# Attention units that own a pair of PSUM banks, batch 0 put into the mixing's tiles, and a priority for every group of operations

## The chip, the cores and the metric

The kernel runs on one core of one Trainium2 chip. The metric is the device time of one execution in microseconds. Three runs of the kernel before took 1059.05, 1060.00 and 1061.12 us, a median of 1060.0 us. The profiled execution took 1059.67 us and its trace spans 1057.9 us; times inside the trace count from the start of that span.

## What is computed

The reference does attention with two kinds of masks, and then a layer that mixes along the sequence and the channels and ends in a feed-forward part. Cut to what matters:

```python
batch, n_heads, seq, head_dim = (8, 8, 576, 64)
# heads 0-3: the last 32 rows; heads 4-7 ("dilated"): every 4th of the last 128 rows
mask_plain = (rel >= 0) & (rel < 32)
mask_dil   = (rel >= 0) & (rel < 128) & (rel % 4 == 0)
x = softmax(where(mask, q @ k.T / 8, -1e9)) @ v          # -> [8, 576, 512]

mixed = real(fft(fft(x, axis=1), axis=2))                # sequence, then channels
u  = x + mixed
un = (u - mean(u)) / sqrt(var(u) + 1e-6)
out = u + maximum(un @ w_ch1, 0) @ w_ch2                 # 512 -> 2048 -> 512
```

## The kernel before

The program is one stream of small operations for TensorE (PE), VectorE (DVE), ScalarE (ACT), GpSimd (POOL) and the DMA queue that SyncE (SP) issues. It has two halves. In the first, about 594 us long, attention, mixing and the feed-forward part of the first six of sixteen blocks of 128 hidden columns run mixed together. In the second, the other ten blocks are done for all tokens by a scheme with seven products in place of eight (`product`, `down7`).

**Attention.** `attention` takes a batch, and in it first the plain heads and then the dilated heads. For each, `loads` brings the keys (`kb`) and the queries (`tq`), and `attend` works through five units `u`: four whole ones of two pairs of heads by four groups of 32 rows, and one half as large. A unit is a chain: scores on PE (L668), masking with the row's extreme on DVE (L677), exponentials on ACT (L683), transposes on PE (L688), a copy to SBUF on ACT (L693), the values on PE (L699), then sum, reciprocal and scaling on DVE (L711, L713, L715) into a tile `xt`, which `store` sends to two DRAM tensors, `xsp` and `xsm` (forward rows and rows counted from the end). All units share the same two banks, held in `split`: the scores of successive units take turns in columns 0 to 127 and 128 to 255, and every unit's values go to columns 256 and up. The transposes take turns in two more banks, `pt` and `av`. In numbers of whole units, a batch has nine and the program 72.

**Mixing.** `mix` does one batch. Its `fold` loads the batch's rows from `xsp` and `xsm` into tiles `x` and `xt` (L802, L811), adds and subtracts them (POOL L814 and L816, DVE L828 and L830, ACT L832 and L833, POOL L836 and L838). Then follow products along the sequence (L865, L887) and along the channels (L911, L917), sums and differences on DVE (L925, L927), the addition of `x` on POOL (`add_u`, L779 and L781), `normalise` (DVE L744 to L756 with a power on POOL L750), and for batch 0 transposes on PE (L764). The result is a tile `ut` of 256 tokens.

**Feed-forward part of the first half.** `fill` takes such a tile through six hidden blocks: `up` (PE L1089, then ACT L1095 and DVE L1097 make `h`), and `down` (PE L1105). There are 18 such tiles, so 108 hidden tiles `h`, each of 12 products up and 6 products down. Their weights arrive as 64-bit floats and are taken apart by `words_of` and `prep` (ACT L991, DVE L993, L996, L999, L1002, ACT L1008, DVE L1009): twelve weight tiles, staged in the four buffers `ut`.

**Hand-over.** Once a batch's memory is free, `blocks` prepares the weights of the second half the same way (tiles `wst`), and stores and reloads many of them through DRAM (`wt`).

**What sets the order.** Nothing is issued in the order in which it is written. Every operation is added to a `Plan` with an engine, a cost, its buffers and a priority; `Plan.run` then simulates the engines, places at each moment the ready operation with the smallest priority number for which buffers are free, and so fixes each engine's instruction order. On the chip each engine follows that order and waits where an input is late. The priorities come from a few constants for each kind of work (`P_QK`, `P_ST`, `P_FILL` and so on).

## Time and profile before

| | |
|---|---|
| runs, median (lowest to highest) | 1060.0 us (1059.05 to 1061.12) |
| profiled execution | 1059.67 us |
| its span | 1057.9 us |
| PE busy | 967.1 us (91%) |
| DVE busy | 838.4 us (79%) |
| ACT busy | 568.2 us (54%) |
| POOL busy | 208.7 us (20%) |
| mean granted TensorE clock | 0.978 |
| moved by DMA | 173.38 MB, mean 164 GB/s |

A busy share is an average over the whole span; the stages differ. The line of the page that shows PE in 40 slices begins 4 3 7 6 6 8 and stays at 9 from the ninth slice on, with one 7. So the time in which PE has nothing to do lies almost all in the first tenth of the span.

### The profile page before, as it was taken

The numbers are of one execution on the slowest core, as the hardware profiler recorded it, in microseconds if no ns is written. First come the engines' busy times: TensorE is split into PE (matmuls) and PEld (weight loads), VectorE is DVE, ScalarE is ACT, GpSimd is POOL, SyncE is SP. The second block draws the span as 40 slices with busy tenths as digits, with TensorE's granted clock in tenths as the row PEclk, the third lists the DMA queues.
The fourth block names the chain that finished last, engine by engine and source line by source line (L and its number), as shares of the span: only waits on it lengthen the run. The fifth ranks groups of instructions, "written<-read, shape, count | busy, mean of one in ns | idle before, by whom it ended". The sixth has DMA issues, their size and how long they took to land.

```text
span 1057.9 us, 29081 instructions
## 1 busy us (share of the span) xinstructions
PE 967.1 (91%) x11092; PEld 880.9 (83%) x11092; DVE 838.4 (79%) x2724; ACT 568.2 (54%) x1476; POOL 208.7 (20%) x278
## 2 busy tenths in 40 slices
PE   4376688989899998999999799999999999999997
PEld 2244476878677897989899699999999999999996
DVE  5469777787867789569987679898989888888787
ACT  3354555364545442325544466667575757575753
POOL 2033324354444536430000000000001000000010
PEclk9999599999999999999999999999999999999999
DMA  9675756888676473346688981322233222223031
GB/s 317 201 262 152 238 183 200 221 254 267 190 243 211 145 230 106 100 141 209 209 266 285 340 285 52 120 67 95 84 98 92 89 87 74 101 61 110 12 103 59
DMA packets 119260, 173.38 MB, mean 164 GB/s; under 512 B 12728, under 2 KB 61112, under 8 KB 119120
## 3 DMA queue, kind: packets, MB, share of 16 engines
q1 hardware_dynamic: 115552, 162.85, 48.6%
q0 software_dynamic: 3040, 8.09, 2.4%
q8 instruction: 87, 1.43, 0.6%
q10 hardware_dynamic: 528, 0.59, 0.2%
q14 instruction: 53, 0.43, 0.1%
HBM read 114.80 MB, written 56.68 MB: 162 GB/s over the span
## 4 chain that ended last, share of the span: by engine, by line
PE 75%; DVE 8%; DMA 4%; issue 1%; ACT 0%; SPq 0%; DVEq 0%; ACTq 0%
PE ff L1457 21%; PE ff L1089 9%; PE ff L1105 9%; PE sc L1567 6%; PE mix L1567 6%; PE av L1567 3%; PE ff L1567 3%; PE pt L1567 3%; PE mix L865 2%; PE sc L1105 2%; PE mix L911 2%; PE sc L699 2%; PE sc L668 2%; DVE pm L677 1%; DMA wt<-wst 1%; PE av L1089 1%
## 5 line engine op out<-in xcount | busy, mean ns | idle before, releaser
L1089 PE MATMUL ff<-ut,wa 128*128 128x256 f32 x936 | 129.9, 288 | 5.0 <-DVE h L1097 5.0
L1089 PEld LDWEIGHTS ff<-ut,wa 128*128 128x128 f32 x936 | 119.4, 192 | 8.6 <-DVE h L1097 5.6
L1147 POOL DMA_INDIRECT ut<-us,flip_sb x20 | 22.4, 1119 | 526.4 <-DVE ut L1168 171.1
L683 ACT ACTIVATE pm<-pm,mx 128x64 f32<-128x64 f32 x288 | 82.6, 342 | 66.3 <-DVE mx L677 64.2
L1105 PE MATMUL ff<-wa,h 128*128 128x512 f32 x468 | 117.9, 399 | 0.0
L1105 PEld LDWEIGHTS ff<-wa,h 128*128 128x128 f32 x468 | 85.1, 189 | 16.7
L677 DVE CUSTOM_DVE_ANT_0 pm<-sc,mask_sb 128x64 f32<-128x64 f32 x288 | 50.9, 217 | 39.4 <-PE sc L668 24.7
L668 PE MATMUL sc<-kb,tq 64*32 64x64 f32 x2304 | 44.1, 256 | 37.4 <-DMA tq<-in_q_dram 19.5
L1457 PE MATMUL ff<-xb,wa 128*128 128x256 f32 x540 | 75.4, 280 | 0.0
L668 PEld LDWEIGHTS sc<-kb,tq 64*32 64x32 f32 x2304 | 29.8, 122 | 53.6 <-issue 18.1
L1457 PE MATMUL ff<-xb,left_w 128*128 128x256 f32 x486 | 69.4, 281 | 0.0
L1457 PE MATMUL ff<-xb,late_w 128*128 128x256 f32 x486 | 68.5, 280 | 0.0
L1457 PEld LDWEIGHTS ff<-xb,wa 128*128 128x128 f32 x540 | 68.4, 188 | 0.1
L1481 ACT ACTIVATE h<-s 128x256 fp32r<-128x256 f32 x134 | 55.0, 417 | 17.4 <-DVE s L1497 12.4
L699 PE MATMUL sc<-vt,ptsb 64*32 64x65 f32 x2304 | 43.9, 246 | 21.8 <-issue 8.5
L699 PEld LDWEIGHTS sc<-vt,ptsb 64*32 64x32 f32 x2304 | 28.7, 117 | 41.6 <-issue 14.0
L1457 PEld LDWEIGHTS ff<-xb,left_w 128*128 128x128 f32 x486 | 62.1, 188 | 0.4
L1457 PEld LDWEIGHTS ff<-xb,late_w 128*128 128x128 f32 x486 | 61.9, 188 | 0.1
L1457 PE MATMUL ff<-xb,right_w 128*128 128x256 f32 x378 | 54.8, 285 | 5.7 <-ACT ys L1465 4.2
L1095 ACT ACTIVATE h<-ff 128x256 fp32r<-128x256 f32 x78 | 29.8, 383 | 52.8 <-PE ff L1089 52.7
L1457 PEld LDWEIGHTS ff<-xb,right_w 128*128 128x128 f32 x378 | 49.4, 193 | 6.9 <-ACT ys L1465 4.4
L1465 ACT COPY s<-ff 128x256 f32<-128x256 f32 x90 | 33.7, 375 | 30.5 <-PE ff L1457 26.2
(252 smaller groups left out, 2525.0 us busy)
## 6 DMA issues: line engine op xcount, KB each, us to landing
vt<-in_v_dram SPq DMA_DIRECT2D x64, 260.0 KB
wst<-in_w_dram SPq DMA_DIRECT2D x20, 512.0 KB
wt<-wst SPq DMA_DIRECT2D x40, 256.0 KB
us<-uc SPq DMA_DIRECT2D x36, 257.0 KB
part<-row SPq DMA_DIRECT2D x36, 256.0 KB
ut<-part SPq DMA_DIRECT2D x36, 256.0 KB
kb<-in_k_dram SPq DMA_DIRECT2D x30, 288.0 KB
ut<-us SPq DMA_DIRECT2D x64, 128.0 KB
```

The costliest lines, as they stand in the source:

```text
L668: nc.tensor.matmul(split[e]()[rows, c0 + KG * c:c0 + KG * c + KG], lhsT=tq()[ps, cols], rhs=kb[j]()[ps, QG * at:QG * at + KG], start=True, ...
L677: nc.vector.tensor_tensor_reduce(pm()[:, i], split[i % 2]()[:, c0 + KG * (i // 2):c0 + KG * (i // 2) + KG], mask_sb()[:, mask_of[dil, u]], ...
L683: add("ACT", 0.25, lambda i=i: nc.scalar.activation(out=pm()[:, i], in_=pm()[:, i], func=AF.Exp, bias=mx()[:, i:i + 1], scale=-1.0), ((mx, ...
L699: nc.tensor.matmul(split[e]()[rows, v0 + 65 * c:v0 + 65 * c + 65], lhsT=pt()[ps, cols], rhs=vt()[ps, at - GS * u, j], start=True, stop=True,)
L1089: nc.tensor.matmul(z()[:, :n_tok], lhsT=wf()[:, a, kk], rhs=ut()[:, p, kk], start=(kk == 0 and n == 0), stop=(kk == KT - 1 and n == 2),)
L1095: add("ACT", act(n_tok) - 0.03, lambda: nc.scalar.activation(out=h()[:, 0, :n_tok], in_=z()[:, :n_tok], func=AF.Relu), (z,), ((h, 0),), prio)
L1105: nc.tensor.matmul(acc(), lhsT=h()[:, a, P * s:P * s + P], rhs=wf()[:, p], start=(first and n == 0), stop=(last and n == 2),)
L1147: add("POOL", 1.3, lambda: nc.gpsimd.indirect_dma_start(u(0, C + 2), None, us[idx // 4](), bass.IndirectOffsetOnAxis(ap=flip_sb()[:, 4 * k ...
L1457: nc.tensor.matmul(up_bank()[:, lo:lo + TOK1], lhsT=ap()[:, a, kk], rhs=xb()[:, j, p, kk], start=(start and k == 0), stop=(k == 5), skip_g ...
L1465: add("ACT", act(n), lambda: nc.scalar.copy(out=dst()[:, 0:n], in_=up_bank()[:, 0:n]), (up_bank, held), (dst,), SOON - 1, urgent=True)
L1481: add("ACT", act(TOK1), lambda: nc.scalar.activation(out=ap()[:, 0], in_=src(), func=AF.Relu if relu else AF.Copy), need, (k0,), prio)
L1567: nc.tensor.matmul(acc()[:, TOK1 * half:TOK1 * half + TOK1], lhsT=ap()[:, a, P * half:P * half + P], rhs=wap()[:, q_].rearrange("p k f -> ...
```

## The change

The constants of the plan are replaced, and eight things change in what is planned:

- The six banks `sc` x2, `pt`, `av`, and so on become `sc` x2, `sd` x2, `mix` x2, `ff` x2. Each attention unit takes a pair of banks (one `sc` and one `sd`), and keeps it from its scores to its scaling: scores in columns 0 to 127 or 255, transposes in columns 256 and up of the first, values over the scores. In batch 0 every other unit takes a `mix` and an `ff` bank instead.
- In batch 0 the dilated heads come first, and the plain heads' units come in the order 2, 4, 3, 0, 1.
- Batch 0's results no longer go to DRAM and back. `direct` sends each `xt` by DMA inside SBUF into the mixing's tiles `x` and `xt`, in pieces that by turns SP and ACT issue, 41 in all.
- For batch 0 the elementwise operations of `fold` and `add_u` run on DVE instead of POOL (26 operations).
- There are nine buffers `vt` (six before), five `tq` (three) and seven `xt` (four).
- Each group of operations (a load, a unit's scores, its tail, a store, a weight tile, a product's hidden tile, and so on) has a number of its own that is added to its priority (`MOVED`), and some a number that is added to their earliest time (`HELD`).
- The plan's figures for costs, the landing of a DMA and its rate are changed a little.
- Masking and exponentials of a unit take the heads of one bank first and then those of the other.

```diff
-NV = 6
-NTQ = 3
+NV = 9
+NTQ = 5
+MOVED = {
+    'x': [2.61, 18.96, 50.59, -57.97, 63.91, 24.37, 48.48, 8, -7.69, 69.28, 26.29, 49.57],
...
+HELD = {
+    'x': [1.59, -28.5, -7.37, 7.5, -0.11, -14.33, -2.44, -2.32, 2.06, 3.04, 0.53, 2.33],
...
     def add(self, eng, cost, fn, r=(), w=(), prio=0.0, nbytes=0, at=0.0, port=False, urgent=False):
+        if self.group is not None:
+            moved = MOVED.get(self.group[0], ())
+            prio += moved[self.group[1]] if self.group[1] < len(moved) else 0.0
+            later = HELD.get(self.group[0], ())
+            at = max(0.0, at + later[self.group[1]]) if self.group[1] < len(later) else at
...
-    banks = {"sc": 2, "pt": 1, "av": 1, "mix": 2, "ff": 2}
+    banks = {"sc": 2, "sd": 2, "mix": 2, "ff": 2}
...
-        for dil in range(2):
+        for n, dil in enumerate((0, 1) if b else (1, 0)):
...
+        split = [bank(t) for t in (("mix", "ff") if b < NOPEN and (dil + u) % 2 else ("sc", "sd"))]
...
-        add("PE", BURST + nh * COST_SC, scores, (tq, *kneed), tuple((x, sc) for x in split), prio)
+        add("PE", BURST + nh * COST_SC, scores, (tq, *kneed), tuple(split), prio)
...
+    def direct(dil, u, xt, prio):
...
+                    puts[0] += 1
+                    on, eng = ((nc.sync, "SP"), (nc.scalar, "ACT"))[puts[0] % 2]
+
+                    def put(dst=dst, cs=cs, ps=ps, rs=rs, on=on):
+                        on.dma_start(out=dst()[rs, cs], in_=xt()[ps, 0:cs.stop - cs.start])
...
+            one = (nc.gpsimd, "POOL", pool) if b else (nc.vector, "DVE", dve)
+            add(one[1], one[2](NEH), lambda: one[0].tensor_tensor(
+                out=t1()[at], in0=xp()[at, 0:NEH], in1=xm()[at, C:C // 2 - 1:-1], op=ALU.add), (xp, xm), (t1,), prio, port=True)
```

How this moves instructions is seen at three places. The first is SP's queue at the end of batch 0's attention. Before: the loads of the next batch, and then the eight loads that bring batch 0's rows back from DRAM.

```order
L584 DMA xsm_68<-blank 1x512
L618 DMA kb_174<-in_k_dram 128x576
L618 DMA kb_175<-in_k_dram 128x576
L632 DMA tq<-in_q_dram 128x512
L802 DMA x_178<-xsp_59 128x512
L802 DMA x_180<-xsp_59 128x512
L802 DMA x_179<-xsm_67 128x512
L802 DMA x_181<-xsm_67 128x512
```

Now, at the same place (L877 is a put into the mixing's tiles, L1147 the load of a weight tile):

```order
L1147 DMA ut<-in_w_dram 128x4x128
L1147 DMA ut<-in_w_dram 128x512
L730 DMA kb_173<-in_k_dram 128x576
L877 DMA xt_181<-xt 32x256
L877 DMA xt_182<-xt 32x256
L877 DMA x_178<-xt 64x128
L692 DMA xsm_69<-in_alt_dram 16x32
L877 DMA x_178<-xt 63x256
```

The loads back have gone; the puts write the tiles themselves, with two weight loads among them.

The second place is DVE where the mixing of batch 0 begins. Before, DVE does only the second half of a fold, between units of batch 1:

```order
L677 ISA pm,mx<-sc,mask_sb 128x64
L677 ISA mx 128x1
L828 TENSOR_TENSOR ee<-t_952,t_961 128x257
L830 TENSOR_TENSOR oo<-t_952,t_961 128x256
L711 TENSOR_SCALAR sums<-sc 128x2 x2
L713 RECIPROCAL rinv<-sums 128x4
L715 TENSOR_TENSOR xt<-sc,rinv 128x2x64 x2
```

Now it does the whole fold, between two weight tiles (L1151 to L1167 are the weights' operations, L967, L969, L981 and L983 the fold's):

```order
L1160 SCALAR_TENSOR_TENSOR ut<-ut 128x512
L1167 TENSOR_TENSOR wa_0_150<-ut,wa_0_150 128x512
L1167 TENSOR_TENSOR wa_0_156<-ut,wa_0_156 128x512
L1151 TENSOR_SCALAR ut<-ut 128x512
L967 TENSOR_TENSOR t_914<-x_177,x_178 128x257
L969 TENSOR_TENSOR t_916<-x_178,x_177 128x257
L1154 SCALAR_TENSOR_TENSOR ut<-ut 128x512
L981 TENSOR_TENSOR ee<-t_914,t_916 128x257
L983 TENSOR_TENSOR oo<-t_914,t_916 128x256
```

The first half of the fold has moved from POOL's list to DVE's, and the units of batch 1 behind it.

The third place is PE at the first product up. Before (432 score and 352 value matmuls, of 16 to a whole unit, stand ahead of it in PE's list):

```order
L668 MATMUL sc<-kb_176,tq 32x64 x4
L668 MATMUL sc<-kb_177,tq 32x64 x4
L688 MATMUL av<-ident_sb,pm 128x128
L764 MATMUL mix<-ident_sb,uc 128x128
L688 MATMUL av<-ident_sb,pm 128x128
L764 MATMUL mix<-ident_sb,uc 128x128 x3
L1089 MATMUL ff<-ut,wa_0_150 128x256 x3
L688 MATMUL pt<-ident_sb,pm 128x128
```

Now (248 score and 232 value matmuls stand ahead of it; L913 is the transpose of the mixing's result, L1250 the product up, L802 a unit's transpose):

```order
L913 MATMUL mix<-ident_sb,uc 128x128 x4
L1250 MATMUL ff<-ut,wa_0_150 128x256 x3
L802 MATMUL sc<-ident_sb,pm 128x128
L1250 MATMUL ff<-ut,wa_0_150 128x256 x3
L781 MATMUL sc<-kb_175,tq 32x64
```

The first product up has moved ahead of eleven and a half units' scores and seven and a half units' values.

## Rows read from the trace of the kernel before

**Rows 1.** Busy time by stage, windows: stretch, length, busy us of each engine

```profile
core 0: us, PE busy (x) PEld busy (x) DVE busy (x) ACT busy (x) POOL busy (x), PEclk, DMA share, GB/s
0.00:128.00 128.00, 71.55 (x1711) 47.41 (x1711) 83.74 (x459) 56.44 (x174) 34.34 (x50) 0.89 0.74 236
128.00:175.00 47.00, 41.72 (x894) 33.12 (x900) 34.93 (x191) 25.71 (x79) 16.66 (x24) 0.93 0.59 180
175.00:594.00 419.00, 403.41 (x4728) 351.85 (x4719) 333.23 (x1184) 195.35 (x533) 137.84 (x187) 1.00 0.68 210
594.00:1058.00 464.00, 450.40 (x3781) 448.49 (x3780) 386.50 (x896) 290.69 (x691) 19.84 (x18) 0.99 0.31 100
```

**Rows 2.** Timeline of PE, end of batch 0's attention: start, us, what, idle before

```profile
24.57 0.62 PE L699 MATMUL sc<-vt,ptsb 64*32 64x65 f32 x16 [2.76 <-issue]
...
37.87 0.88 PE L699 MATMUL sc<-vt,ptsb 64*32 64x65 f32 x32 [0.91 <-DVE xt L715]
40.68 0.83 PE L699 MATMUL sc<-vt,ptsb 64*32 64x65 f32 x32 [1.93 <-issue]
44.81 0.62 PE L699 MATMUL sc<-vt,ptsb 64*32 64x65 f32 x16 [3.29 <-issue]
54.12 1.17 PE L668 MATMUL sc<-kb,tq 64*32 64x64 f32 x64 [8.70 <-DMA tq<-in_q_dram]
```

**Rows 3.** Timelines of DVE, SP's queue and POOL, from batch 0's last scaling to its fold

```profile
46.25 0.36 DVE L715 TENSOR_TENSOR xt<-sc,rinv 128x64 f32<-128x64 f32 x2
...
50.47 0.90 SPq L802 DMA_DIRECT2D x<-xsp  x2
...
56.40 0.72 POOL L814 TENSOR_TENSOR t<-x,x 128x257 f32<-128x257 f32 x1 [30.70 <-DMA x<-xsm]
```

**Rows 4.** Timeline of PE up to the first product up

```profile
106.60 1.13 PE L764 MATMUL mix<-ident_sb,uc 128*128 128x128 f32 x4 [5.92 <-DVE sq L927]
...
127.86 0.99 PE L1089 MATMUL ff<-ut,wa 128*128 128x256 f32 x3
```

**Rows 5.** Groups of DVE until 132 us: busy us, mean ns, idle before

```profile
L677 DVE CUSTOM_DVE_ANT_0 pm<-sc,mask_sb 128x64 f32<-128x64 f32 x108 | 18.5, 219 | 24.2 <-PE sc L668 18.4 <-PE sc L699 5.8
L715 DVE TENSOR_TENSOR xt<-sc,rinv 128x128 f32<-128x128 f32 (+1 forms) x50 | 11.8, 272 | 4.6 <-PE sc L668 4.0 <-DMA xsp<-xt 0.4
L996 DVE SCALAR_TENSOR_TENSOR ut<-ut 128x512 uint32<-128x512 uint32 x11 | 8.0, 731 | 0.1
L711 DVE TENSOR_SCALAR sums<-sc 128x2 f32<-128x2 f32 (+1 forms) x50 | 5.6, 153 | 10.0 <-PE sc L668 6.8 <-PE sc L699 3.1
L830 DVE TENSOR_TENSOR oo<-t,t 128x256 f32<-128x256 f32 (+1 forms) x4 | 1.7, 415 | 0.0
```

**Rows 6.** Timelines of POOL and DVE, an operation beside POOL's additions and one without

```profile
102.16 0.72 POOL L779 TENSOR_TENSOR xrest<-xt,sq 32x257 f32<-32x257 f32 x1
...
102.35 1.08 DVE L996 SCALAR_TENSOR_TENSOR ut<-ut 128x512 uint32<-128x512 uint32 x1
...
132.32 0.42 DVE L1097 SCALAR_TENSOR_TENSOR h<-ff,h 128x256 fp32r<-128x256 f32 x1 [0.28 <-ACT h L1095]
132.66 0.68 DVE L999 SCALAR_TENSOR_TENSOR ut<-ut 128x512 uint32<-128x512 uint32 x1
```

**Rows 7.** Groups of PE from 128 to 594 us: busy us, mean ns, idle before

```profile
L1089 PE MATMUL ff<-ut,wa 128*128 128x256 f32 x936 | 129.9, 288 | 5.0 <-DVE h L1097 5.0
L1105 PE MATMUL ff<-wa,h 128*128 128x512 f32 x468 | 117.9, 399 | 0.0
L699 PE MATMUL sc<-vt,ptsb 64*32 64x65 f32 x1600 | 27.2, 225 | 5.9 <-DVE mx L677 3.9 <-DVE r L754 0.9 <-issue 0.5
L668 PE MATMUL sc<-kb,tq 64*32 64x64 f32 x1440 | 24.6, 227 | 9.1 <-DVE mx L677 4.9 <-DVE xt L715 3.1 <-DVE sums L711 0.8
L688 PE MATMUL pt<-ident_sb,pm 128*128 128x128 f32 x47 | 13.1, 316 | 0.0
```

**Rows 8.** Busy time by stage at the hand-over, windows, columns as in the first group

```profile
480.00:600.00 120.00, 115.33 (x738) 104.61 (x737) 104.43 (x229) 60.47 (x145) 2.54 (x2) 1.00 0.80 262
```

More of the change, by code (lines that the diff above doesn't have):

```diff
@@ L275, in __init__, with turn @@
         self.calm, self.last = False, None
+        self.group, self.seen = None, {}
+    def turn(self, kind):
+        if kind is not None:
+            self.seen[kind] = self.seen.get(kind, -1) + 1
+            kind = kind, self.seen[kind]
+        before, self.group = self.group, kind
+        return before
     def buf(self, pool, tag, shape, dtype, bufs):
@@ L548, in fused_kernel @@
     half = fixed(keep, [P, 1], F32, "half")
-    blank = fixed(heads, [1, C], F32, "blank")
-    split = [plan.buf(lambda: pools["psum"], "sc", [P, 512], F32, banks["sc"]) for _ in range(2)]
-    turn = [0]
     kbs = [fixed(heads, [P, WIN + S], F32, f"kb{i}") for i in range(NKB)]
@@ L733, in store @@
                 n_put += 1
+    puts = [0]
+    def direct(dil, u, xt, prio):
+        step = DIL if dil else 1
+        for back, p0, n, last, row in laid_out(dil, u)[2]:
+            rows = np.arange(row, last + 1, step)
+            home = np.minimum(rows // P, 2) + (rows == S // 2)
+            for at in range(4):
+                mine = np.nonzero(home == at)[0]
+                if not len(mine):
+                    continue
+                dst = xs[2 * at + back] if at < 2 else xtail[back] if at == 2 else xtail[0]
+                r0 = int(rows[mine[0]]) - P * at if at < 3 else 32
+                rs = slice(r0, r0 + step * (len(mine) - 1) + 1, step)
+                for half in range(1 if u < SLOTS else 2):
+                    cs = slice(256 * dil + 128 * half, 256 * dil + (256 if u < SLOTS else 128 * half + 128))
+                    ps = slice(p0 + 2 * QG * half + int(mine[0]), p0 + 2 * QG * half + int(mine[-1]) + 1)
+                    puts[0] += 1
+                    on, eng = ((nc.sync, "SP"), (nc.scalar, "ACT"))[puts[0] % 2]
+                    def put(dst=dst, cs=cs, ps=ps, rs=rs, on=on):
+                        on.dma_start(out=dst()[rs, cs], in_=xt()[ps, 0:cs.stop - cs.start])
+                    add(eng, 0.45, put, (xt,), ((dst, ("put", dil, u, at, back, half)),), prio + P_ST0,
+                        len(mine) * 4 * (cs.stop - cs.start))
     def order(idx):
@@ L795, in fold @@
         def fold(m, prio):
-            early = prio + (P_FD if b else P_FD0)
+            early = prio + P_FD
+            plan.turn("l")
             n = P if m < 2 else 33
@@ L922, in along_channels @@
                         (ps,), (pc,), prio)
+            one = (nc.gpsimd, "POOL", pool) if b else (nc.vector, "DVE", dve)
             at = slice(0, P) if m < 2 else slice(o, o + n)
@@ L1234, in tokens @@
         rows = P * n
+        plan.turn("t")
         tv = tr[1]
@@ L1306, in fill @@
             h = hidden()
-            z = bank(("pt", "av")[f % 2] if late else "ff")
+            z = bank("sd" if late else "ff")
+            plan.turn("u")
             hs.append(up(ut, wa1[f], z, h, prio, TOK1))
+            plan.turn(None)
         if tiles[-1] == NTILE - 1:
```

176 lines of the change are left out of this document (106 added, 70 removed), and 81 rows, old and new, of tables (HELD, MOVED).

## The prediction

> **What bounds the kernel now.** First the busy times by stage [rows 1]: from 594 us to the end PE is busy 450.4 of 464 us and the change leaves its operations there alone, so that part is carried over. From 175 to 594 us PE is busy 403.4 of 419 us and from 128 to 175 us 41.7 of 47: 21 us idle in 466. But in the first 128 us PE is busy 71.6 us only. Everything after that is work that PE does nearly without pause, so the span is the time of PE's work plus what PE loses early, and the question is what the change takes off the opening.
>
> The timelines then say why PE waits early. Batch 0's units stop for 2.76, 1.93 and 3.29 us, each time in front of the values and with no engine as releaser [rows 2]; what values need besides engines' work is `vt`, so I read these as loads that came late because SP's queue asked for them late. Batch 0's last scaling ends at 46.6 us, SP issues the loads of the stored rows at 50.47, and POOL's fold begins at 56.40 [rows 3]: 9.8 us for a trip to DRAM and back. Meanwhile PE stands 8.70 us for the next batch's queries [rows 2]. The mixing's end then runs thin, with one stop of 5.92 us [rows 4]; the first product up, the work that could fill gaps, starts at 127.86 us [rows 4], and its first hidden tile is finished by DVE from 132.32 [rows 6]. DVE is the busiest of the others in this stretch, 83.7 of 128 us [rows 1].
>
> **The change part by part: the opening.** I measure it by the first hidden tile on DVE, at 132.3 us before.
>
> DVE's list up to that tile. By the two orders it loses 42 of 108 masks (18.5/108 = 0.171 us each, 7.2), 18 of 50 sums (0.112, 2.0) and 18 of 50 scalings (0.236, 4.2), with nine reciprocals, which I price like sums (1.0): 14.4 us less [rows 5]. It gains the 26 additions that were POOL's, at 0.415 us like the nearest DVE addition of that width (10.8), and one more weight tile of five operations at 8.0/11 = 0.73 us (3.6): 14.4 us more [rows 5]. So the list is as long as before: 83.7 us until 128 plus about 3.2 for the next four (34.93/47 a us), 87 us [rows 1]. One thing gets cheaper: with POOL out of batch 0's mixing, operations like the L996 that took 1.08 us beside a POOL addition take the 0.68 us of the L999 without one [rows 6]. The mean of 0.731 [rows 5] says this is 0.05 us an operation over 60 weight operations, 3 us. That leaves 84 us.
>
> The Trainium skill (GPSIMD Engine Reference, 1. Specifications) says that GpSimd's SBUF interfaces are shared with VectorE, with contention for VectorE operations of two SBUF inputs, and (4.1 Engine selection) names VectorE as the engine for elementwise work. The trace agrees on both: 0.72 us for an addition on POOL, 0.415 on DVE, and 1.08 against 0.68 beside one [rows 5, 6].
>
> When DVE can begin on it. Batch 0's attention needs 36 masks, 18 sums, 9 reciprocals and 18 scalings, with the first memsets some 16 us of the 84. It ended at 46.6 us. The three stops of 8.0 us together go: in the new order all ten `vt` loads of batch 0 stand among SP's first eighteen rows, and nine buffers hold them. Four units in flight instead of waits like the 0.91 us for a scaling [rows 2] give some 2 to 3 us more. So it ends near 36 us, and the first weight tiles are there for DVE to work on until the puts land. The other 68 us of DVE's list then follow without a long hole, since ten weight tiles fill what the mixing's chain leaves: first hidden tile at 36 + 68 = **104 us**, 28.3 us earlier. Bounds: attention done at 32 us and contention gone wholly (62 us of list), 94; attention done at 40 and DVE idle a tenth of the time, 40 + 75 = 115.
>
> What ACT pays: it issues 21 of the 41 puts in batch 0. At the 0.45 us that SP takes for an issue (0.90 for two [rows 3]) that is 9.5 us of an engine that is busy 56.4 of 128 us [rows 1]; I count nothing, and up to 3 us in the bound of 40 us.
>
> **What PE then has left.** Ahead of the first product up, PE's list loses 184 score matmuls (11.5 units), 120 value matmuls (7.5 units), 22 transposes and a transpose of the mixing. They come later, when PE is the bound. The trace records a score or value matmul as two, so 1440 and 1600 are 45 and 50 units: 24.6/45 = 0.55 us a unit's scores, 27.2/50 = 0.54 a unit's values, and 13.1/47 = 0.28 a transpose [rows 7]: 6.3 + 4.1 + 6.4 = 16.8 us. They also bring the waits of attention with them, 9.1 + 5.9 us for 45 units [rows 7], 0.33 a unit: 3.8 us. Given back: **20.6 us**, bounds 16.8 and 25.
>
> **Banks of their own.** Of PE's waits after 128 us, 3.1 us were for a scaling and 0.8 us for a sum [rows 7], that is for banks still being read. A pair that belongs to one unit removes that sharing, and puts a new wait in its place: only two pairs are left after batch 0, so the third unit's scores wait for the first unit's scaling, and behind those scores PE's whole list waits, products up and down too. Best 4 us gained; worst under the rivals. I take **2 us gained**, since two units cover a batch of nine in the 50 us that it gets.
>
> **The hand-over.** Where the second batch of weights is taken apart, the order has 39 hidden tiles left for PE before and 36 now, with the same DVE work. Three tiles are 3 x (12 x 129.9/936 + 6 x 117.9/468) = 9.5 us of cover [rows 7]. DVE was idle 15.6 of 120 us there [rows 8] because PE was the bound; so most of the lost cover comes out of that idle time. I take **1 us lost**, bounds 0 and 9.5.
>
> Everything else (the other batches' priorities, the order of masks and exponentials, the buffers) has no price of its own in the rows: 21 us of idle time after 128 us [rows 1] is what the priorities could gain or, if the planned times are wrong, enlarge. I take nothing, and keep 8 us either way.
>
> **The sum**, against the profiled execution of 1059.67 us, which is the median of 1060.0 within 0.4: 1059.67 - 28.3 + 20.6 - 2 + 1 = 1051.0 us. A difference under about 0.2%, 2.1 us, could not be told from none.
>
> **The rivals.**
> 1. *The opening gives more.* DVE's list shrinks to the undisturbed 62 us and the attention of batch 0 ends at 32 us; PE finds products to fill with from 91 us on. For it: batch 0's stops were all for loads; POOL's additions disturb DVE visibly [rows 6]. Against it: the chain of the mixing still needs DVE, PE and ACT in turn. 94 in place of 104 gives 1041 us; with half of the 21 us of later idle time gone as well, 1031. The sharing of interfaces that the Trainium skill states in GPSIMD Engine Reference, 1. Specifications, is the mechanism; it is a case of this rival, and the one row pair bears it out.
> 2. *Nothing is left of it.* What is given back and the hand-over cost their upper bounds, 25 and 9.5 us, with no gain of banks: 1059.67 - 28.3 + 25 + 6 would be 1062, with half of the hand-over 1059. For it: DVE is busy 104.4 of 120 us at the hand-over [rows 8], so less cover means that DVE is late. Against it: part of its idle time there can still be used.
> 3. *Two pairs are too few: slower.* After the first product up 56.5 units remain. If each second one finds its pair still in use and stops PE for the 0.91 us that such a wait took in the opening [rows 2], it costs 28 x 0.91 = 25 us, and the 2 us of banks are not gained: 1078; at half that wait, 1066. It decides from 0.18 us a unit on (the 10 us of the sum over 56 units). For it: PE executes in order, and masks already make PE wait 4.9 and 3.9 us [rows 7]. Against it: in a 50 us batch a unit can take 11 us before two pairs run out, and products stand between.
> 4. *The direct puts don't bring the fold forward*, because the weight tiles that stand ahead of it in DVE's list, or a put behind a waiting one on SP or ACT, come late. Then the fold starts as before at 56 us, DVE works off weights meanwhile, and the first hidden tile comes at 115 or later: 1062 us.
>
> **How the numbers follow.** The forecast's own case, 1042 to 1058, has 0.45; the first rival 0.20; the second 0.12, half of it within 0.2%; the third 0.17; the fourth 0.06, the most of it slower or the same. Faster by over 0.2%: 0.66. Within 0.2%: 0.12. Slower by over 0.2%: 0.22. The range reaches from the first rival's far case to the half-priced third: 1031 to 1067.
>
> **What would show it.** In the new trace: batch 0's last scaling near 36 us (32 to 40) and no wait over 1 us for a `vt`; the fold's first addition on DVE within 5 us of it; DVE idle under a tenth from there to the first hidden tile at 104 us (94 to 115); PE idle in the first 128 us some 30 us less than 56; after it, attention's waits on PE of 15 to 20 us in all and none over 1 us for a scaling; the first product of the second half at 585 us instead of 594, and 464 us from it to the end. The forecast is wrong where the first hidden tile comes after 115 us, where PE loses more than 40 us between it and the second half, or where the second half itself is longer by more than 2 us.

## The result, and the profile after

The changed kernel takes 1049.9 us (median of four runs, 1044.5 to 1052.0) against 1059.8 for the kernel before, a ratio of 0.9897 with a 95% interval of 0.9859 to 0.9936: 10 us faster, 1.1 us from the forecast. The profiled execution took 1050.0 us, its span is 1048.2. The total came out as predicted; the way to it did not. The stages, against [rows 1]:

```profile
core 0: us, PE busy (x) PEld busy (x) DVE busy (x) ACT busy (x) POOL busy (x), PEclk, DMA share, GB/s
0.00:128.00 128.00, 74.95 (x1549) 54.87 (x1557) 91.44 (x446) 54.07 (x157) 8.61 (x18) 0.91 0.71 225
128.00:175.00 47.00, 45.10 (x955) 36.68 (x955) 33.00 (x201) 25.16 (x84) 23.73 (x34) 1.00 0.72 218
175.00:582.00 407.00, 389.69 (x4823) 336.85 (x4822) 329.32 (x1208) 193.80 (x545) 134.74 (x182) 0.99 0.69 212
582.00:1048.00 466.00, 453.11 (x3781) 451.06 (x3779) 386.70 (x897) 290.18 (x691) 19.84 (x18) 0.98 0.31 101
```

PE's idle time in the first 128 us fell from 56.5 to 53.1 us only, although DVE is 7.7 us busier there and POOL nearly free. The marks of the opening (timelines of DVE and PE; start, us, what):

```profile
45.84 0.28 DVE L829 TENSOR_TENSOR xt<-ff,rinv 128x128 f32<-128x128 f32 x1
...
50.35 0.42 DVE L967 TENSOR_TENSOR t<-x,x 128x257 f32<-128x257 f32 x1
...
103.75 0.99 PE L1250 MATMUL ff<-ut,wa 128*128 128x256 f32 x3
...
108.82 0.41 DVE L1259 SCALAR_TENSOR_TENSOR h<-ff,h 128x256 fp32r<-128x256 f32 x1
```

Batch 0's last scaling ends at 46.1 us, no earlier than before ([rows 3], 46.6). The fold begins 4.2 us after it instead of 9.8, the first product up comes at 103.75 instead of 127.86 [rows 4], and the first hidden tile at 108.8 instead of 132.3 [rows 6]. The groups of PE from 104 to 582 us answer to [rows 7] (busy us, mean ns, idle before):

```profile
L1250 PE MATMUL ff<-ut,wa 128*128 128x256 f32 x936 | 134.9, 290 | 3.3 <-DVE h L1259 1.4 <-ACT row L1285 1.4 <-DVE ve L895 0.5
L1267 PE MATMUL ff<-wa,h 128*128 128x512 f32 x468 | 122.0, 403 | 1.3 <-DVE h L1259 1.3
L1250 PE MATMUL sd<-ut,wa 128*128 128x256 f32 x360 | 46.7, 285 | 4.7 <-DVE h L1259 4.7
L813 PE MATMUL sc<-vt,ptsb 64*32 64x65 f32 x920 | 28.1, 224 | 2.8 <-issue 1.7 <-ACT ptsb L807 1.0
L802 PE MATMUL sc<-ident_sb,pm 128*128 128x128 f32 x115 | 28.0, 287 | 3.0 <-ACT pm L797 2.8
L781 PE MATMUL sc<-kb,tq 64*32 64x64 f32 x904 | 27.6, 225 | 2.1 <-DVE xt L829 1.8 <-PE sc L802 0.2
```

The waits for masks are gone, and one wait of 1.8 us for a scaling is left. Ahead of the second half PE now stands for hidden tiles: 4.5 of the 4.7 us in the `sd` row are two stops, at 495 and 567 us. The 5.0 us of the same kind before ([rows 7], L1089) lay earlier, at 146, 402 and 420 us.

### The profile page after: what moved, and what is told of

The parts are those of the page before. It is cut to its first block, busy times and chain, and to the rows that moved or that the text cites. A ratio compares the mean times of both kernels' runs of the same rounds, so it can differ in the third digit from the quotient of the medians.

```text
span 1048.2 us, 29205 instructions
## 1 busy us (share of the span) xinstructions
PE 962.8 (92%) x11092; PEld 879.5 (84%) x11092; DVE 840.5 (80%) x2751; ACT 563.2 (54%) x1476; POOL 186.9 (18%) x252
## 4 chain that ended last, share of the span: by engine, by line
PE 73%; DVE 12%; DMA 8%; ACT 3%; issue 2%; SPq 1%; POOL 0%; ACTq 0%; DVEq 0%; POOLq 0%
PE ff L1624 22%; PE ff L1250 8%; PE ff L1267 7%; PE sc L1734 6%; PE sd L1734 6%; PE mix L1734 6%; PE mix L1066 3%; PE ff L1734 3%; PE sd L1250 3%; PE mix L1019 2%; PE sc L813 2%; PE sc L781 1%; DMA wst<-in_w_dram 1%; DMA ut<-us 1%; PE sc L802 1%
## 5 line engine op out<-in xcount | busy, mean ns | idle before, releaser
L1250 PE MATMUL ff<-ut,wa 128*128 128x256 f32 x936 | 134.9, 290 | 3.3 <-DVE h L1259 1.4
L1250 PEld LDWEIGHTS ff<-ut,wa 128*128 128x128 f32 x936 | 119.5, 191 | 9.4 <-DVE h L1259 2.3
L1267 PE MATMUL ff<-wa,h 128*128 128x512 f32 x468 | 122.0, 403 | 1.3 <-DVE h L1259 1.3
L797 ACT ACTIVATE pm<-pm,mx 128x64 f32<-128x64 f32 x288 | 79.5, 339 | 76.8 <-DVE mx L791 58.3
L1648 ACT ACTIVATE h<-s 128x256 fp32r<-128x256 f32 x134 | 55.3, 417 | 20.3 <-DVE s L1664 15.4
L1624 PEld LDWEIGHTS ff<-xb,right_w 128*128 128x128 f32 x378 | 51.3, 199 | 6.6 <-ACT ys L1632 3.0
L1250 PEld LDWEIGHTS sd<-ut,wa 128*128 128x128 f32 x360 | 45.5, 192 | 6.7 <-DVE h L1259 5.5
L1250 PE MATMUL sd<-ut,wa 128*128 128x256 f32 x360 | 46.7, 285 | 4.7 <-DVE h L1259 4.7
L791 DVE CUSTOM_DVE_ANT_0 pm<-sc,mask_sb 128x64 f32<-128x64 f32 x135 | 26.1, 218 | 29.9 <-PE sd L781 28.1
L781 PE MATMUL sc<-kb,tq 64*32 64x64 f32 x1080 | 36.3, 237 | 13.6 <-DMA tq<-in_q_dram 5.1
L781 PEld LDWEIGHTS sc<-kb,tq 64*32 64x32 f32 x1080 | 24.4, 112 | 26.6 <-issue 19.2
```

Of the source, the lines that this page charges most:

```text
L781: nc.tensor.matmul(split[e]()[rows, KG * c:KG * c + KG], lhsT=tq()[ps, cols], rhs=kb[j]()[ps, QG * at:QG * at + KG], start=True, stop=True,)
L791: nc.vector.tensor_tensor_reduce(pm()[:, i], split[i % 2]()[:, KG * (i // 2):KG * (i // 2) + KG], mask_sb()[:, mask_of[dil, u]], -0.125, 3 ...
L797: add("ACT", 0.25, lambda i=i: nc.scalar.activation(out=pm()[:, i], in_=pm()[:, i], func=AF.Exp, bias=mx()[:, i:i + 1], scale=-1.0), ((mx, ...
L1250: nc.tensor.matmul(z()[:, :n_tok], lhsT=wf()[:, a, kk], rhs=ut()[:, p, kk], start=(kk == 0 and n == 0), stop=(kk == KT - 1 and n == 2),)
L1267: nc.tensor.matmul(acc(), lhsT=h()[:, a, P * s:P * s + P], rhs=wf()[:, p], start=(first and n == 0), stop=(last and n == 2),)
L1624: nc.tensor.matmul(up_bank()[:, lo:lo + TOK1], lhsT=ap()[:, a, kk], rhs=xb()[:, j, p, kk], start=(start and k == 0), stop=(k == 5), skip_g ...
```

## Why batch 0's attention ends no earlier

Timelines of SP, ACT, PE and DVE of the changed kernel, from 11 to 33 us (a row of several goes from the start of its first to the end of its last):

```profile
11.48 5.80 SPq L758 DMA_DIRECT2D vt<-in_v_dram  x5
17.37 1.55 SPq L877 DMA_DIRECT2D x<-xt  x2
18.98 0.72 SPq L877 DMA_DIRECT2D xt<-xt  x1
19.75 2.42 SPq L745 DMA_DIRECT2D tq<-in_q_dram  x2
24.02 0.33 SPq L730 DMA_DIRECT2D kb<-in_k_dram  x1
...
20.77 0.94 ACTq L877 DMA_DIRECT2D x<-xt  x1
24.40 2.42 ACTq L877 DMA_DIRECT2D x<-xt  x4
28.90 0.67 ACTq L877 DMA_DIRECT2D xt<-xt  x1
29.66 2.39 ACTq L877 DMA_DIRECT2D x<-xt  x3
32.16 1.06 ACT L797 ACTIVATE pm<-pm,mx 128x64 f32<-128x64 f32 x4 [11.45 <-DMA x<-xt]
...
26.66 0.39 PE L781 MATMUL sc<-kb,tq 64*32 64x64 f32 x2 [5.08 <-DMA tq<-in_q_dram]
...
29.27 0.23 DVE L791 CUSTOM_DVE_ANT_0 pm<-sc,mask_sb 128x64 f32<-128x64 f32 x1 [6.15 <-PE sd L781]
```

What SP's queue waited for until 34 us (us, times, longest), and all puts of the kernel by queue (ns: shortest/middle/longest):

```profile
SPq L758 <- DMA tq<-in_q_dram: 2.4, 2, 2.2
SPq L758 <- DMA vt<-in_v_dram: 2.0, 2, 1.0
SPq L758 <- DMA x<-xt: 1.9, 1, 1.9
```

```profile
L877 ACTq DMA_DIRECT2D x<-xt x16: 488/602/1107, 10.7 to 46.2; - x16
L877 SPq DMA_DIRECT2D x<-xt x13: 514/625/962, 17.4 to 44.3; - x13
```

The stops for `vt` are gone as forecast, and DVE is done with the dilated heads at 23.1 us. But SP issues the plain heads' queries, at 19.75, behind their five `vt` loads and three puts of the first unit. That unit's scaling had ended at 10.6 us, so the puts waited for their turn in the queue and not for a result. The `vt` loads ahead of them stood some 6 us for the landings of earlier transfers. So the plain heads' first masks come at 29.3; and their exponentials only at 32.2, because ACT issues nine puts first. Of ACT's 11.45 us without work the nine issues are 6.2. In between ACT stands 2.7 and 2.1 us, until 24.40 and 28.90, each time for an earlier transfer that lands at 24.38 and 28.88. In this trace the transfers of SP and ACT use the same eight semaphores in turn, and at each of these waits the next issue goes out when the last transfer with its semaphore has landed. ACT's 21 issues together take 14.6 us, 0.70 in the mean, where I had counted 0.45 and no cost.

The first experiments keep the changed kernel's own order, held fixed, and edit one or two things in it. The table has all twelve: median, ratio to the kernel before in the same comparison, and marks in us from each trace (end of batch 0's last scaling, fold's first addition, first product up, first product of the second half, span).

| kernel | us | ratio (95%) | scaling | fold | up | 2nd half | span |
|---|---|---|---|---|---|---|---|
| before | 1059.8 | | 46.6 | 56.4 | 127.9 | 594.1 | 1057.9 |
| changed | 1049.9 | 0.9897 (0.9859 to 0.9936) | 46.1 | 50.4 | 103.8 | 582.0 | 1048.2 |
| u1_q_first | 1051.5 | 0.9931 (0.9912 to 0.9950) | 45.9 | 50.2 | 103.6 | 582.9 | 1048.1 |
| u2_q_pool_puts | 1043.6 | 0.9868 (0.9824 to 0.9912) | 37.7 | 41.9 | 94.2 | 573.5 | 1040.7 |
| u3_pool_adds | 1053.2 | 0.9937 (0.9910 to 0.9963) | 47.0 | 49.1 | 107.2 | 585.6 | 1051.3 |
| u4_tiles_first | 1047.1 | 0.9893 (0.9858 to 0.9929) | 46.8 | 51.1 | 103.3 | 584.5 | 1045.0 |
| u5_dram | 1064.1 | 1.0038 (1.0013 to 1.0064) | 42.5 | 60.8 | 115.3 | 596.8 | 1062.3 |
| u6_no_tables | 1051.0 | 0.9916 (0.9898 to 0.9935) | 41.3 | 49.0 | 110.2 | 569.5 | 1044.2 |
| u7_shared_banks | 1113.8 | 1.0492 (1.0472 to 1.0512) | 49.8 | 51.3 | 117.2 | 622.4 | 1117.2 |
| u8_before_numbers | 1036.3 | 0.9767 (0.9741 to 0.9793) | 45.3 | 55.3 | 111.9 | 567.8 | 1033.8 |
| u9_numbers_pool_puts | 1031.3 | 0.9740 (0.9671 to 0.9809) | 42.9 | 51.2 | 108.4 | 564.5 | 1030.3 |
| u10_before_banks | 1036.2 | 0.9762 (0.9705 to 0.9818) | 43.0 | 55.0 | 130.0 | 570.2 | 1036.7 |
| u11_replanned | 1022.6 | 0.9640 (0.9597 to 0.9684) | 34.4 | 46.0 | 107.8 | 556.9 | 1019.9 |
| u12_dram_replanned | 1028.1 | 0.9705 (0.9679 to 0.9731) | 35.9 | 51.2 | 116.2 | 563.0 | 1025.8 |

Medians of one kernel scatter by some us, so differences of a few are read from the marks.

**u1_q_first.** After planning, the second keys and both queries of the plain heads (operations 177 to 179) are put ahead of their first `vt` (180).

```diff
+MOVES = [((178, 179, 177), 180)]
...
+        for nums, before in MOVES:
+            order = hoisted(self, order, nums, before)
         for o in order:
             o.fn()
```

> The changed kernel in its own order, with three loads moved: the queries and keys of batch 0's plain heads are issued on SP ahead of the plain heads' values, not behind the first three puts. Theory A (two stops in series): the plain heads start late for two reasons, the queries (PE's 5.1 us stop until 26.66 us, DVE's until 29.27) and then ACT, which issues puts until 32.0 us ahead of their exponentials. Then this alone moves the first plain masks from 29.3 to about 23 us, but the exponentials stay at 31 to 32 us, batch 0's last scaling at 45 to 46 and the first hidden tile at 105 to 107; time within 2 us of 1049.9. Theory B (the loads alone): the whole chain comes 5 to 6 us earlier, last scaling at 40 us, first hidden tile at 100 to 101, time 1045 to 1047.

(The 106.6 us given there and below for the changed kernel's first hidden tile was misread; its row stands at 108.8.) Theory A: the queries come in time and DVE's stop of 6.15 us is gone, yet the exponentials start as late as ever, so no mark moves by more than a microsecond. Timeline of ACT:

```profile
29.93 1.94 ACTq L910 DMA_DIRECT2D x<-xt  x3
31.98 1.06 ACT L830 ACTIVATE pm<-pm,mx 128x64 f32<-128x64 f32 x4 [10.60 <-DMA xt<-xt]
```

**u2_q_pool_puts.** The same, and GpSimd issues ACT's puts at the same places.

```diff
-                    on, eng = ((nc.sync, "SP"), (nc.scalar, "ACT"))[puts[0] % 2]
+                    on, eng = ((nc.sync, "SP"), (nc.gpsimd, "ACT"))[puts[0] % 2]
```

> As the kernel with the three loads first, and the 21 puts of batch 0 that ACT issues are issued by GpSimd at the same place in the order. Theory A (two stops in series, both gone): exponentials of the plain heads from 24 us, last scaling at 36 to 39 us, the fold's first addition at 41 to 45 instead of 50.4, first hidden tile at 96 to 101 instead of 106.6; of these 6 to 10 us some half comes back as later work of PE, so 1043 to 1047 us. Theory B (the queue of the puts is no matter): as the kernel with the loads alone. Theory C: GpSimd's puts land later than ACT's and the fold starts no earlier than 50 us; time as the changed kernel or 2 to 4 us over it.

Theory A, with its last clause wrong. The last scaling comes at 37.7 us, the fold 8.4 us earlier, the first product up 9.6 and the second half 8.5: nothing is given back on the way. Work is displaced by an order, not by being early; in one and the same order the gain of the opening arrives whole. GpSimd takes 0.52 us a put (its timeline):

```profile
23.99 1.03 POOL L910 DMA_DIRECT2D x<-xt  x2
25.01 0.52 POOL L910 DMA_DIRECT2D xt<-xt  x1
26.06 1.55 POOL L910 DMA_DIRECT2D x<-xt  x3
```

The Trainium skill (DMA: Bandwidth & Descriptors, Issuing engines are not separate DMA queues) says that issuing from several engines saves only the sequencer's time, usually small beside the transfer. For a single put the trace agrees: 0.60 us on ACT, while ten of GpSimd's puts, those whose landing the trace tells, land 2.6 to 7.7 us after their issue. But ACT pays it 21 times, with the waits for landings on top, while batch 0's exponentials stand behind; freeing ACT of both was worth 8 us of the kernel (u1 against u2). The run does not tell the issues from the waits, since on GpSimd the puts use semaphores of their own; and the puts on GpSimd without the three loads moved were not tried.

**u3_pool_adds.** The 26 additions go back to GpSimd, in the changed kernel's order.

```diff
-            one = (nc.gpsimd, "POOL", pool) if b else (nc.vector, "DVE", dve)
+            one = (nc.gpsimd, "POOL", pool) if b else (nc.gpsimd, "DVE", dve)
```

> The changed kernel in its own order, with the 26 additions of batch 0's mixing that it put on DVE issued by GpSimd again. Theory A (DVE's list is the bound of the opening, as the prediction reckoned it): DVE loses 26 x 0.415 = 10.8 us and pays 3 us of disturbance, so the first hidden tile comes 5 to 8 us earlier than 106.6. Theory B (the mixing's chain is the bound and DVE works it off faster): 26 x (0.72 - 0.415) = 8 us of chain more and DVE's weight operations at 0.73 instead of 0.68 us, first hidden tile 4 to 10 us later, time 1052 to 1058.

Theory B, at a smaller size: the first product up 3.5 us later, the second half 3.6. DVE waits 4.2 + 2.5 us for POOL's results, and the weight operations beside them take 718 and 776 ns (L1154, L1167) instead of 684 and 682; POOL's additions take up to 1054 ns. My list of DVE counted the additions as 10.8 us of work; their worth is that the chain no longer changes engines and that the weight operations beside it run undisturbed.

**u4_tiles_first.** Two waiting hidden tiles (operations 4031 and 4037) go ahead of the weight operation 4377.

```diff
+MOVES = [((4031, 4037), 4377)]
```

> The changed kernel in its own order, but near 563 us DVE finishes two waiting hidden tiles ahead of five weight operations instead of behind them. Theory A (the hand-over lost time by the order alone): PE's stop of 3.4 us at 563 to 566 us falls under 1.5 us, the first product of the second half comes 2 to 3 us before 581.8, time 1045 to 1048. Theory B (DVE's work up to the second half decides): the stop goes, but PE waits as much longer just before the second half, whose first product stays within 1 us of 581.8; time within 1 us of 1049.9.

Neither theory. The second half begins 2.5 us later than in the changed kernel, but takes 460.5 us instead of 466.2. Windows of its first 31 us, the changed kernel's first:

```profile
581.99:612.99 31.00, 25.52 (x177) 24.29 (x176) 17.38 (x40) 14.58 (x36) 0.00 (x0) 0.83 1.01 363
```

```profile
584.50:615.50 31.00, 27.92 (x225) 26.74 (x224) 20.93 (x50) 19.79 (x48) 0.00 (x0) 1.00 1.00 356
```

In the changed kernel PE stops for 3.4, 1.5 and 2.7 us around the start of the second half and is granted 0.83 of the full 2.4 GHz over the window (1.2 GHz for 10.2 us from 585.2 on, and the full clock for the rest); here it stops for 2.5 and 1.8 us, the clock is granted in full, and 48 more matmuls fit into the window, which holds 2.4 us more of busy time. So in these two executions the hand-over cost the changed kernel more than its idle time shows. The run times do not tell the kernels apart (ratios 0.9893 and 0.9897).

**u5_dram.** Batch 0's rows go through DRAM again, in the changed kernel's order; the fold's first addition issues seven loads first.

```diff
+                    far = (xsm if back else xsp)[0]
...
-                        on.dma_start(out=dst()[rs, cs], in_=xt()[ps, 0:cs.stop - cs.start])
+                        on.dma_start(out=far()[there, cs], in_=xt()[ps, 0:cs.stop - cs.start])
...
+                    nc.sync.dma_start(out=x()[p0:p0 + hi - lo, 0:C], in_=src()[lo:hi])
```

> The changed kernel in its own order, but batch 0's 41 puts go to the two stores in DRAM, and seven loads on SP bring the rows into the mixing's tiles right ahead of the first addition of each fold, as the kernel before had it. Theory A (the direct puts bring the fold forward, and DVE, which is never idle afterwards, carries that to the end): from the last scaling to the fold 9 to 10 us instead of 4.2, as before; fold at 55 to 57, first hidden tile 113 to 115, second half from 587 to 588, time 1053 to 1056. Theory B (the trip through DRAM is hidden by the weight operations ahead of the fold): fold within 2 us of 50.4 and time within 2 us of 1049.9.

In direction theory A, at over twice its size: the second half begins 14.8 us later. But it is one load that holds up the fold (timelines of SP and DVE, the load's size, and a window of 1 us):

```profile
45.70 0.29 SPq L975 DMA_DIRECT2D x<-xsm  x1
...
60.84 0.43 DVE L976 TENSOR_TENSOR t<-x,x 128x257 f32<-128x257 f32 x1 [14.02 <-DMA x<-xsm]
...
x<-xsm SPq DMA_DIRECT2D x1, 254.0 KB
50.30:51.30 1.00, 0.00 (x0) 0.00 (x0) 0.00 (x0) 0.00 (x0) 0.00 (x0) 1.00 0.07 27
```

The edit loads 127 rows there (254 KB), since row 0 is zeroed by DVE; the kernel before loads 128. The load issued at 45.70 lands at 60.75, 15 us later. The load of 128 rows issued at 44.95 lands at 50.29, and the kernel before's four take 4.4 to 5.4 us. In the window the DMA share of 0.07 is that of one of the 16 DMA engines, busy with packets of 2048 bytes one after the other. So the run shows what a load of 127 rows costs on this chip, and does not decide between its theories; what the trip through DRAM costs is read from u12.

## What the parts are worth in orders of their own

From here on the planner makes a new order for each kernel, so a difference is that of the part and of all that the order does with it.

**u6_no_tables** and **u8_before_numbers.** Without the two tables; u8 has the single numbers of before as well.

```diff
-MOVED = {
...
-HELD = {
...
+MOVED, HELD = {}, {}
```

> The changed kernel without the two tables of numbers for its groups of operations; everything else is kept, and the planner makes a new order. Theory A (the tables are what keeps PE's later waits down): the opening stays within 5 us of the changed kernel's (first hidden tile 104 to 113), and between the first product up and the second half PE waits 30 us or more instead of 19.7; time 1058 to 1075. Theory B (banks, puts and additions bring the gain, and the tables little): time 1047 to 1054. Theory C (the opening's order is in the tables): first hidden tile after 115 us, DVE idle over 8 us between the fold and the first product up instead of 1.6; time over 1058 for that reason.

> The changed kernel without the two tables, and with all of the planner's single numbers as they were before: banks, puts, additions on DVE, buffers and batch 0's order of heads alone. Theory A (the structure brings the gain): the fold is as early as 48 to 52 us, the first hidden tile at 104 to 113, time 1047 to 1056. Theory B (structure and numbers only work together): PE waits over 30 us between the first product up and the second half; time 1058 to 1080, so that the structure alone would be no gain over the 1060 of before.

u6 fits theory B in the total. u8 is 13.6 us faster than the changed kernel with every number of it undone, more than its theory A, and not for the reason that A gave: its fold is late, at 55.3 us. The marks say where the time is (u6's are from an execution 5 us under its median). Both reach the second half at 568 to 570 us, the changed kernel at 582.0; u8 then needs 466.0 us, u6 474.7, the changed kernel 466.2. So its single numbers cost the second half 8.7 us (u6 has a stop of PE of 7.0 us there, at 604 us, for a weight reloaded from DRAM), and the tables win that back and lose 12.5 us in the first half. In u8 the first product up comes 8 us later than in the changed kernel, and the time from there to the second half is 22 us shorter: an early first product is no aim in itself when attention's work is put off for it. Which of the numbers does it was not tried.

**u10_before_banks.** The kernel before, with a pair of banks for each unit and nothing else.

```diff
-    banks = {"sc": 2, "pt": 1, "av": 1, "mix": 2, "ff": 2}
+    banks = {"sc": 2, "sd": 2, "mix": 2, "ff": 2}
...
+        split = [bank(t) for t in (("mix", "ff") if b < 1 and (dil + u) % 2 else ("sc", "sd"))]
...
-                        split[e]()[rows, c0 + KG * c:c0 + KG * c + KG], lhsT=tq()[ps, cols],
+                        split[e]()[rows, KG * c:KG * c + KG], lhsT=tq()[ps, cols],
```

> The kernel before with one part of the change alone: every attention unit has its own pair of banks (in batch 0 every second unit the pair of the mixing and the products), its turned probabilities in the first of them. Loads, stores, additions and all numbers are those of before, and the planner makes a new order. Theory A (own pairs are a large part of what the structure brings): the waits of scores and values for masks, scalings and sums, 12.7 us after the first product up, mostly go, and batch 0 ends earlier; time 1044 to 1053. Theory B (the prediction's price): 2 us or less, time 1056 to 1062. Theory C (two pairs stop PE more often than shared banks do): over 1063.

Better than theory A: 1036.2 us, as much as u8 with all other parts of the change. The first product up is no earlier (130.0); from there to the second half it takes 440.2 us instead of 466.2. PE's waits in that stretch, the kernel before first (waited for: us, times, longest):

```profile
PE ff L1089 <- DVE h L1097: 5.0, 3, 1.8
PE sc L668 <- DVE mx L677: 4.9, 12, 0.8
PE sc L699 <- DVE mx L677: 3.9, 9, 0.6
PE sc L668 <- DVE xt L715: 3.1, 5, 0.9
PE sc L699 <- DVE r L754: 0.9, 1, 0.9
PE sc L668 <- DVE sums L711: 0.8, 2, 0.5
```

```profile
PE ff L1099 <- DVE h L1091: 1.8, 1, 1.8
PE sc L663 <- issue: 1.6, 2, 1.0
PE ff L1083 <- DVE h L1091: 1.3, 1, 1.3
PE mix L859 <- POOL ees L830: 0.7, 2, 0.4
```

The 12.7 us of waits for masks, scalings and sums are gone, and since nothing but the banks was edited I read them all as waits for banks that DVE was still reading; PE's idle time in the stretch falls from 20.9 to 7.0 us. Its busy time falls by another 12 us. Some 4 us of that are accounted for: five units' values moved ahead of the stretch, and a unit's scores take 22.7/44 = 0.52 (rows of both banks together) instead of 24.6/45 = 0.55 us. Why the operations stand tighter is not settled. Nor is how much of the gain is the planner's. The values go to columns 256 and up and yet wait 3.9 us for masks, which read columns 0 to 255 of the same bank; the plan of the kernel before keeps these groups of columns apart, so it planned no such wait. Planning them with shared banks was not tried.

**u7_shared_banks.** The converse: the changed kernel with the shared banks of before.

```diff
-    banks = {"sc": 2, "sd": 2, "mix": 2, "ff": 2}
+    banks = {"sc": 2, "pt": 1, "av": 1, "mix": 2, "ff": 2}
```

> The changed kernel with the banks of before: all units write their scores and values into two shared banks, the turned probabilities go to two more, and batch 0 has no pair of its own in the mixing's banks; tables and numbers are kept, and the planner makes a new order. Theory A (own pairs save waits): PE waits 6 us or more in all for scalings, sums and masks in front of scores and values after the first product up, against 1.8 us now, and batch 0's last scaling comes 2 us or more later than 46; time 1055 or more. Theory B (the prediction's 2 us or less): those waits stay under 4 us and the time within 4 us of 1049.9, unless the new order itself loses time elsewhere, which PE's list of waits would show.

Theory A in direction: PE waits 25 us for sums, scalings and masks after 105 us. But the second half is 29 us longer too, where no attention is left, so these 29 of the 64 us at least are not waits for banks. The tables, applied to an order that they were not made for, are the likely cause; no run tests it. As a price of the banks only u10 counts.

**u9_numbers_pool_puts.** u8's order with the two edits of u2, the loads ahead of the weights' (operation 1758).

```diff
+MOVES = [((176, 177, 178, 179), 1758)]
...
+                    on, eng = ((nc.sync, "SP"), (nc.gpsimd, "ACT"))[puts[0] % 2]
```

> The structure of the change with the single numbers of before and no tables, in that kernel's own order (1036.3 us), with two edits: the two keys' and two queries' loads of batch 0's plain heads are issued ahead of the first two loads of weights, and the 21 puts that ACT issues are issued by GpSimd at the same place. Theory A (the stops of batch 0's plain heads cost here as they did in the changed kernel): last scaling at 37 to 40 us instead of 45.3, fold at 46 to 51 instead of 55.3, first product up at 103 to 108 instead of 111.9, second half from 560 to 565 instead of 567.8; time 1028 to 1033. Theory B (this order fills the opening with attention of the next batches, so an earlier fold brings nothing): first product up within 3 us of 111.9, time 1034 to 1038. Theory C (the weights now come late and DVE waits for them): time over 1038.

Theory A by its time, 1031.3 us, but the marks gain only 2.4 to 4.1 us. The weights that the loads overtook come late, and DVE, with their first operation ahead of attention's in its list, waits 9.24 us for them until 23.5 us.

**u11_replanned.** u8 with both edits known to the planner: the loads are not held back, and every second put is GpSimd's.

```diff
-T_LD = [-7.5, 10.45, 12.81, -0.43, -9.07, -6.97]
+T_LD = [-7.5, 0, 12.81, -0.43, -9.07, -6.97]
...
-                    on, eng = ((nc.sync, "SP"), (nc.scalar, "ACT"))[puts[0] % 2]
+                    on, eng = ((nc.sync, "SP"), (nc.gpsimd, "POOL"))[puts[0] % 2]
```

> The structure of the change with the single numbers of before and no tables, and two edits that the planner knows of this time: the loads of batch 0's plain heads are not held back, and every second put of batch 0 is GpSimd's, not ACT's; the planner makes a new order. Theory A (attention of batch 0 without the stops of its plain heads, and without DVE waiting 9.2 us for weights as in the last run): last scaling at 36 to 41 us, fold at 41 to 48, first product up at 98 to 106, second half from 552 to 561, time 1018 to 1028. Theory B (what an early fold brings is given back as later work of PE): the opening as in A, but the second half from 561 to 566 and 1028 to 1033. Theory C (GpSimd's tables and puts in one queue hold each other up): seq or chn tables late, the fold or the first seq product over 52 us, time over 1033.

Theory A, but for a first product up 2 us later than it said: 1022.6 us, 3.6% under the kernel before and the fastest of all. Batch 0's last scaling ends at 34.4 us, inside the 32 to 40 that the prediction gave for an opening without stops. Its stages up to the end:

```profile
0.00:45.97 45.97, 16.47 (x594) 11.00 (x594) 26.68 (x168) 18.06 (x54) 16.96 (x35) 0.73 0.97 302
45.97:107.77 61.80, 43.28 (x1014) 30.32 (x1015) 59.01 (x296) 34.55 (x105) 7.45 (x10) 0.69 0.81 255
107.77:449.90 342.13, 333.99 (x5028) 285.02 (x5029) 270.79 (x1182) 170.30 (x496) 151.00 (x208) 1.00 0.67 201
449.90:556.90 107.00, 106.87 (x679) 96.86 (x678) 98.04 (x214) 54.47 (x132) 6.04 (x2) 1.00 0.80 258
556.90:1019.90 463.00, 450.48 (x3781) 448.33 (x3779) 386.19 (x895) 292.27 (x691) 21.35 (x19) 0.99 0.31 100
```

From the first product up to the second half PE is idle 8.3 us of 449; DMA is busy 0.97 of the time until the fold, against 0.80 in the changed kernel, so in the opening the loads leave little more to gain.

**u12_dram_replanned.** u11 without the direct puts.

```diff
-        if b == 0:
-            direct(dil, u, xt, prio)
-            return
...
-                for x, src in ((xp, plus), (xm, minus)) if b else ():
+                for x, src in ((xp, plus), (xm, minus)):
```

> The kernel of 1022.6 us without the direct puts: SP writes batch 0's rows to the two stores in DRAM (30 puts in place of 41) and loads them back for the fold, as the kernel before did; own banks, additions on DVE, the heads' order, the unheld loads and all numbers stay, and the planner makes a new order. Theory A (the direct puts bring the fold forward and PE keeps it): fold from 51 to 56 us instead of 46.0, first product up 4 to 8 us after 107.8, time 1026 to 1031. Theory B (the planner fills the trip with weight operations, and what is early in the opening is given back later): fold over 50 us, but first product up and second half within 3 us of 107.8 and 556.9, time 1020 to 1026. Own pairs alone made 1036 of 1060; by A the direct puts are worth 4 to 9 us of the rest, by B nothing.

Theory A: fold 5.2 us later, second half 6.1, time 5.5 us more, though the intervals of the two ratios just overlap. So the direct puts are worth 5 to 6 us, once they don't hold up the attention that feeds them. With ACT issuing them, all parts of the structure but the banks brought nothing in sum (u8 against u10).

## Right and wrong, step by step

**Opening, right by accident.** Batch 0's end was to be at 36 us and was 46.1. The step that failed is the one that let the stops go: it saw the loads of `vt` among SP's first rows and did not look at what stood behind them and SP's first puts (the plain heads' queries and keys), and it priced ACT's puts at nothing, where ACT was not done with them before 32.1 us. The rest made up for part of it: from the last scaling to the first hidden tile I had 68 us and it took 62.7, the "62 us of list" that I kept for the first rival, with weight operations at 0.68 us throughout and DVE busy 51.8 of the 53.4 us from the fold to the first product up. First hidden tile 108.8, inside 94 to 115; the gain 23.5 us instead of 28.3.

**Given back, too dear.** From the first product up to the second half the changed kernel takes 478.2 us, 12.0 more than before. I had 20.6 less 2 for the banks plus 1 for the hand-over, 19.6. PE's busy time there is 13.2 us more (I had 16.8). Its idle time is 19.7 us against 20.9, made of other things: the waits for banks gone, new waits come.

**Own banks, the worst-sized term.** I took 2 us, at best 4, because I counted the waits for scalings and sums [rows 7] as waits for banks, and read the 8.8 us for masks in the same rows as a sign of in-order execution, in favour of the third rival. They are the same kind: DVE still reads the bank that PE wants to write. u10 measures 24 us (by its interval 19 to 31), of which 12.7 are those waits. Two pairs were not too few: one wait of 1.8 us for a scaling, none other.

**Hand-over, undersized.** 1 us taken; the trace has 5 us more of idle time ahead of the second half (in 120 us that reach 5.5 us into it PE is busy 110.6, against 115.3 in [rows 8]), and the second half itself, which I had left unchanged, is 2.4 us longer. The bound of 9.5 held.

**The priorities, not priced at all.** "I take nothing, and keep 8 us either way": the new numbers cost 13.6 us (u8 against the changed kernel). This and the banks' gain are the two errors that cancel in the total, by luck. By the parts in their own orders the change was worth 24 us, and the numbers took 14 back. Stage by stage, by the marks of the table, it is 24.1 us gained up to the first product up, 12.0 given back and 2.4 lost in the second half, 9.7 in all; I had 28.3, 19.6 and nothing.

**Of the signs named ahead**, these held: no wait for a `vt`, fold within 5 us of the last scaling, DVE idle under a tenth, first hidden tile in its bounds. PE's idle time in the first 128 us fell by 3.4 us, not 30: what attention left there was not filled. Attention's waits after it are 7.9 us, under the 15 to 20 forecast, and one of them, the 1.8 us for a scaling, is over the 1 us named. The second half begins at 582.0, not 585, and takes 466.2 us, 0.4 past the bound at which I called the forecast's working wrong. The rivals: the first one's means were there (the undisturbed list) and batch 0's late end kept them from showing; the second, third and fourth did not come about. What the fourth rested on, work held up in the queues of SP and ACT, was there, but it delayed attention and not the fold. The second rival's sum was wrong: with the upper bounds that it names, 25 and 9.5 us, it gives 1065.9 us and not 1062.

## What to carry to other kernels

A wait of PE for VectorE in front of a write to PSUM can be a bank shared by two pieces of work, whatever VectorE is doing with it; adding such waits up under one heading would have pointed at 12.7 of the 24 us here. A small transfer costs the engine that issues it 0.5 to 0.7 us, and what it stands for earlier transfers to land; so it belongs on an engine that nobody waits for, and a load that is needed soon belongs ahead of transfers that can wait. A timeline's row of several issues is not all issuing: it can hold pauses. Numbers that steer an order are to be tried at their old values whenever the structure changes: here the structure alone gained over twice what the tuned whole did.

## What the runs showed of the hardware

A put takes its issuing engine about as long on each of the three: 0.60 us in the middle on ACT (at most 1.22), 0.63 on SP and 0.53 on GpSimd (u2), where SP's larger loads take 0.45 [rows 3]. ACT and SP also stand for landings of earlier transfers: ACT 2.7 and 2.1 us in the changed kernel, SP's five `vt` loads some 6 us.

A load of 127 rows of 2048 bytes landed after 15 us, and the DMA share was 0.07, one engine of 16, while nothing else was moving; loads of 128 such rows landed after 4.1 to 5.4 us (u5, and the kernel before).

A pause of PE can be followed by a lower granted clock that costs as much as the pause: at the start of the second half 0.83 over 31 us in the changed kernel, 1.00 in u4, and 5.7 us between the two second halves, of which 2.4 are idle time. The length of the stop alone does not tell: in the kernel before, a stop of 4.2 us that ends at 599.8 was accompanied by 3.4 us at 1.2 GHz, and the same window there was granted 0.94. In the opening a lower clock works against a shorter stretch: in u2 the mixing's stretch is granted 0.60 where the changed kernel had 0.81, and yet it is 1.1 us shorter, since DVE and not PE bounds it there (DVE busy 51.7 of 52.3 us).
